# Softmax denominators of an attention and FFN kernel: products with 64 columns of ones, or with 32 columns and the queries in two strips

## The chip, the core and the metric

The kernel runs on one core of one Trainium2 chip. The metric is the device time of one execution, in microseconds (us). Before the change it is 1072.7 us, the median of 3 runs (1072.04 to 1073.84).

A core has a matrix engine (TensorE, in the profile PE, its weight loads PEld), VectorE (DVE), ScalarE (ACT) and GpSimd (POOL). TensorE multiplies a stationary operand (lhsT) with a moving one (rhs) and leaves the result in PSUM. The stationary operand's columns become the partitions of the result, so a product whose result has 64 partitions uses 64 of the array's 128 columns.

## What is computed

The reference is an attention in which a query sees only keys that are assigned to the same centroid, and then a bilinear FFN on its output:

```python
# q, k, v: (4, 8, 768, 64); centroids: (8, 16, 64)
mask = q_assign[:, :, :, None] == k_assign[:, :, None, :]
scores = scale * np.matmul(q, k.transpose(0, 1, 3, 2))
scores = np.where(mask, scores, -1000000000.0)
scores = scores - np.max(scores, axis=-1, keepdims=True)
attn = np.exp(scores)
attn = attn / (np.sum(attn, axis=-1, keepdims=True) + 1e-09)   # <- the denominators
x = np.matmul(attn, v)               # (4, 8, 768, 64) -> (3072, 512)
out = ((x @ w_a) * (x @ w_b)) @ w_out     # 512 -> 1536 -> 512
```

There are 4 batches, 8 heads and 768 queries. The change concerns the sum over the keys in `attn` and its reciprocal.

## The kernel before

The kernel treats two heads (a = 0, 1) and half of the queries (HB = 384) at a time: 16 head pairs p, two halves hf each, so 32 groups of denominators. HP = 4 head pairs make a batch. A unit is one tile of 128 keys; six units make a half. The steps of several head pairs and of the FFN are interleaved by hand, in one static order for each engine.

The probabilities lie with the keys on the partitions and the queries along the free dimension. Their sum over the keys is therefore a sum over units, done by VectorE and GpSimd, and then a sum over partitions, done by a product with ones on TensorE. Numbers such as L572 are the lines of the kernel that the profile names.

```python
ones = c["ones"] = const.tile([P, D], FP32, name="ones")      # P = 128, D = 64
nc.vector.memset(ones, 1.0)
...
# exponentials, L524; probabilities pt have 4 buffers, score tiles s in PSUM 2
pt = ptp.tile([P, 2, HB], FP32, name="pt")
nc.scalar.activation(out=pt, in_=s[:, :, 0:HB], func=AF.Exp, scale=SCALE)
...
def add_up(u):                                        # the sum over units
    p, hf, j = where(u)
    if j == 0 or j == NJ - 1 and p < HP:              # first batch: the last unit
        return                                        # is left to TensorE
    if j == 1:
        accs[p, hf] = accp.tile([P, 2, HB], FP32, name="acc")     # 2 buffers
    acc = accs[p, hf]
    for a in range(2):
        many = p >= HP and (a == 1 or j in (2, 4))
        eng = nc.gpsimd if many else nc.vector
        eng.tensor_tensor(out=acc[:, a, :],                                # L538
            in0=probs[u - 1][:, a, :] if j == 1 else acc[:, a, :],
            in1=probs[u][:, a, :], op=ALU.add)

def weigh(us):                                        # the product with v
    ...
            for a in range(2):
                nc.tensor.matmul(out=O_of[0][a * D:(a + 1) * D, 0:HB],     # L549
                                 lhsT=vs[p][:, a, j, :], rhs=probs[u][:, a, :],
                                 start=(j == 0), stop=(j == NJ - 1))

def denominators(p, hf):
    ps = ps_m.tile([P, 512], FP32, name="m")          # PSUM, 3 buffers
    acc = accs.pop((p, hf))
    terms = [acc]
    if p < HP:                                        # first batch: two terms
        terms.append(probs[p * UPP + hf * NJ + NJ - 1])
    for n, t in enumerate(terms):
        for a in range(2):
            nc.tensor.matmul(out=ps[a * D:(a + 1) * D, 0:HB], lhsT=ones,   # L572
                             rhs=t[:, a, :], start=(n == 0),
                             stop=(n == len(terms) - 1))
    den = acc[:, 0, :]
    nc.scalar.activation(out=den, in_=ps[:, 0:HB], func=AF.Copy,           # L577
                         accum_out=stat[:, n:n + 1])
```

All 64 rows of a head's result are alike, for all columns of the stationary operand are ones. `normalize` needs the reciprocal of each query's denominator on all 64 partitions of the head. It takes one reciprocal for each query instead of 64: VectorE's transpose works on blocks of 32x32, so after it a query's denominator stands in one column of a block, and only that column is inverted; the transpose back of the broadcast reciprocals spreads them over the block again.

```python
def across():
    nc.vector.transpose(out=once, in_=den)                                 # L592
def invert():
    nc.vector.reciprocal(out=inv,                                          # L595
        in_=once.rearrange("p (j t) -> p j t", t=32)[:, :, 0])
def back():
    nc.vector.transpose(out=den,                                           # L599
        in_=inv[:, :, None].broadcast_to((P, HB // 32, 32)))
def apply():
    nc.gpsimd.tensor_tensor(out=x, in0=x, in1=den, op=ALU.mult)            # L604
    ...
return [across, invert, back, apply]
```

The four steps are put into the order of the engines one at a time, each behind a piece of the FFN's products (if there is any at that time):

```python
denominators(*divmod(g // 3 - 1, 2))       # in every third group of two units
...
if halved:
    todo.extend(normalize(*ph))
...
    while len(ffn) > least and credit > 0:
        cost, piece = ffn.popleft()
        credit -= cost
        piece()                            # products of L632, L732 or L851
        if todo:
            todo.popleft()()
```

A step of the preparation of the next head pair, the similarities to the centroids, stands close by on TensorE. It already uses 32 columns of the array four times side by side:

```python
def prep_sim(p):
    ps = ps_m.tile([P, 512], FP32, name="m")
    for kq in range(4):
        nc.tensor.matmul(out=ps[32 * kq:32 * kq + 32, 0:HB],               # L353
                         lhsT=cTb[:, hp, :],                               # 128 x 32
                         rhs=qkTs[p][:, kq * HB:(kq + 1) * HB],
                         start=True, stop=True)
```

Other lines that the text names: L367 transposes these similarities on TensorE in the first batch; L428 transposes queries and keys on VectorE (768 columns); L742 adds an FFN product to its sum on VectorE; L715 combines weights on VectorE, for the FFN's products follow a scheme with fewer products and more sums; L113 is a reciprocal of one element per partition; L976 is a pair of small VectorE instructions, one for partitions 0 to 63 and one for 64 to 127.

Of the kernel before, what the change touches and what calls it, by code (L numbers as in the profile page):

```python
# [13 lines left out]
AF = mybir.ActivationFunctionType  # L14
ALU = mybir.AluOpType
# [20 lines left out]
def kernel(  # L36
# [89 lines left out]
    with ExitStack() as fast:  # L126
        short_path(nc, tc, fast, c, cn, centroids_in, casts, n_far, q, k, v,
                   moe_w_a, moe_w_b, moe_w_out, out)
# [8 lines left out]
def short_path(nc, tc, ctx, c, cn, centroids_in, casts, n_far, q, k, v,  # L137
# [3 lines left out]
    B, H, S, D = q.shape  # L141
# [5 lines left out]
    NCH = DM // P  # L147
    NF = DF // P
    HB = S // 2

    def pool(name, bufs, space=None):
        kw = {} if space is None else {"space": space}
        return ctx.enter_context(tc.tile_pool(name=name, bufs=bufs, **kw))
# [21 lines left out]
    ident, identb, ones, rank = c["ident"], c["identb"], c["ones"], c["rank"]  # L175
# [171 lines left out]
    def prep_sim(p):  # L347
# [4 lines left out]
        for kq in range(4):  # L352
            nc.tensor.matmul(out=ps[32 * kq:32 * kq + 32, 0:HB],  # L353
                             lhsT=cTb[:, hp, :],
                             rhs=qkTs[p][:, kq * HB:(kq + 1) * HB],
                             start=True, stop=True)
        if by_blocks(p):
            sims[p] = ps
            return
        t = simp.tile([P, HB], FP32, name="sim")  # L360
        nc.scalar.copy(out=t, in_=ps[:, 0:HB])
        sims[p] = t
# [48 lines left out]
    def prep_by_blocks(p):  # L411
# [19 lines left out]
        def sims_across():  # L431
            v.transpose(out=sim.rearrange("p g c -> p (g c)"),
                        in_=sims[p][:, 0:HB])

# [8 lines left out]
        def one_hot_across():  # L443
            v.transpose(out=ohT, in_=oh.rearrange("p g c -> p (g c)"))
            for a in range(2):
                for kq in range(4):
                    r = 32 * kq + a * NC
                    nc.sync.dma_start(
                        out=ohTs[p][a * D:a * D + NC, kq * HB:(kq + 1) * HB],
                        in_=ohT[r:r + NC, :])  # L450
# [111 lines left out]
    def denominators(p, hf):  # L562


        ps = ps_m.tile([P, 512], FP32, name="m")
        acc = accs.pop((p, hf))
        terms = [acc]
        if p < HP:
            terms.append(probs[p * UPP + hf * NJ + NJ - 1])
        for n, t in enumerate(terms):  # L570
            for a in range(2):
                nc.tensor.matmul(out=ps[a * D:(a + 1) * D, 0:HB], lhsT=ones,  # L572
                                 rhs=t[:, a, :], start=(n == 0),
                                 stop=(n == len(terms) - 1))
        den = acc[:, 0, :]
        n = 4 * p + 2 * hf
        nc.scalar.activation(out=den, in_=ps[:, 0:HB], func=AF.Copy,  # L577
                             accum_out=stat[:, n:n + 1])
        den_of[p, hf] = acc

    def normalize(p, hf):

        b, hp = divmod(p, HP)
        acc = den_of.pop((p, hf))
        den, once = acc[:, 0, :], acc[:, 1, :]
        x = xTs[b][:, hp, hf * HB:(hf + 1) * HB]
        inv = small.tile([P, HB // 32], FP32, name="inv")

        def across():
            nc.vector.transpose(out=once, in_=den)  # L592

        def invert():
            nc.vector.reciprocal(  # L595
                out=inv, in_=once.rearrange("p (j t) -> p j t", t=32)[:, :, 0])

        def back():
            nc.vector.transpose(  # L599
                out=den,  # L600
                in_=inv[:, :, None].broadcast_to((P, HB // 32, 32)))

        def apply():
            nc.gpsimd.tensor_tensor(out=x, in0=x, in1=den, op=ALU.mult)  # L604
            unchecked.append((4 * p + 2 * hf + 1, inv))

        return [across, invert, back, apply]

    def check_inverses():
        while unchecked:  # L610
# [376 lines left out]
    for g in range(NG + 3):  # L987
        p, l = divmod(g, GPP)
# [16 lines left out]
        if g % 3 == late and 0 < g - late:  # L1005
            denominators(*divmod(g // 3 - 1, 2))
# [15 lines left out]
        if halved:  # L1022
            todo.extend(normalize(*ph))
# [24 lines left out]
    def some_ffn(n):  # L1048
        for _ in range(n):
# [15 lines left out]
    ps = ps_m.tile([P, 512], FP32, name="m")  # L1065
    nc.tensor.matmul(out=ps[0:1, 0:1], lhsT=far_off, rhs=ones[:, 0:1],
                     start=True, stop=True)
# [227 lines left out]
```

## Time and profile before

The profile is of one execution, with a span of 1071.4 us and a mean granted TensorE clock of 0.995.

| part of the profile | number |
|---|---|
| VectorE busy | 713.7 us |
| L572, products with ones, TensorE | 160 records |
| L592 and L599, VectorE's transposes | 32 each, 566 and 575 ns mean |
| L595, VectorE's reciprocal | 32, 221 ns mean |
| L577, ScalarE's copy of the denominators | 32, 488 ns mean |
| L604, GpSimd's product | 32, 1039 ns mean |
| L353, similarities, TensorE | 128 records |

How to read it: a record of TensorE is busy from the issue of a product to its modelled end, and records overlap, so that the busy time of a line of TensorE counts the same moment more than once. What a group of products costs is the distance between its first start and the first start of the next group. An fp32 product leaves two records. On VectorE, an instruction that waits for nothing can start a little before the one ahead of it has ended. "Idle before, releaser" names the instruction whose end let a waiting one go on.

### The profile page before, as it was taken

How to read it: one execution, taken by the hardware profiler on the slowest of the kernel's cores; microseconds unless marked ns; L12 is line 12 of the kernel's file. 1: busy time of each engine (PE TensorE's matmuls, PEld its weight loads, DVE VectorE, ACT ScalarE, POOL GpSimd, SP SyncE). 2: the span in 40 equal slices, each digit the busy share in tenths (PEclk: the TensorE clock that was granted, in tenths of full speed). 3: DMA queues.
4: the chain of work that ended last, by engine and by line, in shares of the span. 5: the costliest groups of instructions: out<-in, count | busy, mean ns of one | idle time of the engine just before them, and what ended most of it. 6: DMA issues, size and time to landing. Idle time of an engine off the chain costs nothing.

```text
span 1071.4 us, 13000 instructions
## 1 busy us (share of the span) xinstructions
PE 1046.6 (98%) x4719; PEld 602.5 (56%) x4719; DVE 713.7 (67%) x1396; ACT 259.0 (24%) x500; POOL 355.8 (33%) x329
## 2 busy tenths in 40 slices
PE   5999999999999999999999999999999999999997
PEld 3444455454556665454545766455455687555686
DVE  5888978787857537766666746667665745676762
ACT  4565423333322221122121221221212200000000
POOL 1221244454542323434444522344344410222200
PEclk8999999999999999999999999999999999999999
DMA  4335352525120120202030030300000000000001
GB/s 140 91 83 91 90 123 82 123 83 136 66 49 15 31 53 14 45 4 45 2 45 2 24 65 13 56 1 19 1 4 1 6 30 25 0 1 1 0 30 33
DMA packets 120504, 46.18 MB, mean 43 GB/s; under 512 B 106608, under 2 KB 115824, under 8 KB 120432
## 3 DMA queue, kind: packets, MB, share of 16 engines
q1 hardware_dynamic: 119456, 43.40, 17.9%
q10 hardware_dynamic: 976, 1.87, 0.5%
q8 instruction: 39, 0.64, 0.3%
q14 instruction: 33, 0.27, 0.1%
HBM read 37.78 MB, written 6.29 MB: 41 GB/s over the span
## 4 chain that ended last, share of the span: by engine, by line
PE 93%; DVE 5%; issue 0%; DMA 0%; POOL 0%; ACT 0%; DVEq 0%; POOLq 0%
PE m L732 30%; PE m L851 19%; PE O L549 12%; PE m L632 12%; PE s L517 11%; PE s L508 4%; PE m L572 3%; PE m L353 1%; DVE raw L693 1%; PE m L337 1%; DVE raw L715 1%; DVE xT L693 0%; DVE acc L538 0%; PE m L399 0%; DVE size L693 0%
## 5 line engine op out<-in xcount | busy, mean ns | idle before, releaser
L524 ACT ACTIVATE pt<-s 128x768 f32<-128x768 f32 x192 | 145.3, 809 | 313.7 <-PE s L517 258.5
L538 POOL TENSOR_TENSOR acc<-acc,pt 128x384 f32<-128x384 f32 x144 | 151.9, 1068 | 59.8 <-ACT pt L524 43.5
L747 POOL TENSOR_TENSOR h<-h,ha 128x384 f32<-128x384 f32 x72 | 72.6, 1016 | 235.8 <-DVE ha L742 234.3
L549 PE MATMUL O<-pt,v 128*64 128x384 f32 x768 | 145.1, 499 | 0.0
L517 PE MATMUL s<-qkT 64*128 64x384 f32 x768 | 140.7, 486 | 0.0
L742 DVE TENSOR_TENSOR ha<-ha,m 128x384 f32<-128x384 f32 x126 | 66.8, 546 | 74.1 <-PE m L732 73.3
L742 DVE TENSOR_TENSOR h<-h,m 128x384 f32<-128x384 f32 x126 | 67.4, 549 | 68.5 <-PE m L732 67.7
L538 DVE TENSOR_TENSOR acc<-acc,pt 128x384 f32<-128x384 f32 x96 | 72.8, 787 | 35.4 <-POOL acc L538 35.0
L549 PEld LDWEIGHTS O<-pt,v 128*64 128x64 f32 x768 | 46.6, 136 | 86.4 <-issue 82.1
L604 POOL TENSOR_TENSOR xT<-xT,acc 128x384 f32<-128x384 f32 x32 | 33.3, 1039 | 169.7 <-DVE acc L599 139.2
L517 PEld LDWEIGHTS s<-qkT 64*128 64x128 f32 x768 | 71.1, 188 | 32.0 <-issue 0.6
L851 PE MATMUL m<-wo_sb,h 128*128 128x256 f32 x384 | 87.5, 382 | 0.0
L851 PEld LDWEIGHTS m<-wo_sb,h 128*128 128x128 f32 x384 | 72.1, 190 | 16.0 <-issue 4.2
L732 PE MATMUL m<-raw 128*128 128x384 f32 x192 | 70.2, 488 | 0.9 <-DVE ha L742 0.9
L632 PE MATMUL m<-xT,wa_sb 128*128 128x384 f32 x192 | 67.1, 492 | 0.0
L632 PE MATMUL m<-xT,wb_sb 128*128 128x384 f32 x192 | 66.8, 491 | 0.0
L851 PE MATMUL m<-xT,h 128*128 128x256 f32 x288 | 65.4, 382 | 0.1
L851 PEld LDWEIGHTS m<-xT,h 128*128 128x128 f32 x288 | 54.1, 190 | 11.7 <-issue 1.7
L732 PE MATMUL m<-xT,wa_sb 128*128 128x384 f32 x144 | 53.0, 491 | 0.0
L732 PE MATMUL m<-xT,size 128*128 128x384 f32 x144 | 52.9, 490 | 0.0
L732 PE MATMUL m<-xT,wb_sb 128*128 128x384 f32 x144 | 52.9, 490 | 0.0
L632 PEld LDWEIGHTS m<-xT,wa_sb 128*128 128x128 f32 x192 | 35.5, 190 | 29.4 <-issue 3.6
(159 smaller groups left out, 1446.4 us busy)
## 6 DMA issues: line engine op xcount, KB each, us to landing
raw<-in_moe_w_out_dram SPq DMA_DIRECT2D x12, 512.0 KB, 3.4
raw<-in_moe_w_a_dram SPq DMA_DIRECT2D x11, 512.0 KB, 3.8
raw<-in_moe_w_b_dram SPq DMA_DIRECT2D x11, 512.0 KB, 3.6
qk<-in_q_dram SPq DMA_DIRECT2D x48, 96.0 KB, 3.1
qk<-in_k_dram SPq DMA_DIRECT2D x48, 96.0 KB, 3.6
v<-in_v_dram SPq DMA_DIRECT2D x24, 192.0 KB, 3.9
out_dram<-rest SPq DMA_DIRECT2D x24, 128.0 KB, 1.7
ohT<-oh SPq DMA_DIRECT2D x96, 12.0 KB, 1.8
```

The lines of the kernel that those rows point to most:

```text
L508: nc.tensor.matmul(out=s[:, a, 0:HB], lhsT=ohTs[p][r, S + j * P:S + (j + 1) * P], rhs=ohTs[p][r, hf * HB:(hf + 1) * HB], start=True, stop= ...
L517: nc.tensor.matmul(out=s[:, a, 0:HB], lhsT=qkTs[p][r, S + j * P:S + (j + 1) * P], rhs=qkTs[p][r, hf * HB:(hf + 1) * HB], start=False, stop ...
L524: nc.scalar.activation(out=pt, in_=s[:, :, 0:HB], func=AF.Exp, scale=SCALE)
L538: eng.tensor_tensor(out=acc[:, a, :], in0=probs[u - 1][:, a, :] if j == 1 else acc[:, a, :], in1=probs[u][:, a, :], op=ALU.add)
L549: nc.tensor.matmul(out=O_of[0][a * D:(a + 1) * D, 0:HB], lhsT=vs[p][:, a, j, :], rhs=probs[u][:, a, :], start=(j == 0), stop=(j == NJ - 1))
L572: nc.tensor.matmul(out=ps[a * D:(a + 1) * D, 0:HB], lhsT=ones, rhs=t[:, a, :], start=(n == 0), stop=(n == len(terms) - 1))
L604: nc.gpsimd.tensor_tensor(out=x, in0=x, in1=den, op=ALU.mult)
L632: nc.tensor.matmul(out=ps[:, 0:HB], lhsT=w_sb[:, ch, f * P:(f + 1) * P], rhs=xTs[b][:, ch, t0:t0 + HB], start=(ch == 0), stop=(ch == NCH - 1))
L732: nc.tensor.matmul(out=ps[:, 0:HB], lhsT=A[l][c], rhs=rhs[c], start=(c == 0), stop=(c == 1))
L742: nc.vector.tensor_tensor(out=out, in0=in0, in1=ps, op=op)
L747: nc.gpsimd.tensor_tensor(out=to, in0=to, in1=box[name], op=ALU.mult)
L851: nc.tensor.matmul(out=ps[:, 0:HN], lhsT=A[l][f // 3][:, f % 3, :], rhs=B[r][f // 2][:, f % 2, :], start=(f == 0), stop=(f == N2 - 1))
```

## The change

The denominators are computed with 32 columns of ones instead of 64. Each head's 384 queries are cut into two strips of QB = 192, and the four products (two heads, two strips) go to four quarters of the array's columns. The result then has 128 partitions of 192 columns: head 0 in quarters 0 and 1, head 1 in quarters 2 and 3. It is meant to shorten the products with ones on TensorE.

What follows has to match. ScalarE's copy and the first transpose have 192 columns. The reciprocals of a strip have to reach both quarters of the head's partitions, so that the transpose back still has 384 columns on all 64 partitions of the head: instead of one reciprocal of 128x12 there are eight of 32x6, for each head from each of two quarters to each of two quarters. They form two steps of four, one step for each head, so that a normalization has five steps instead of four.

```diff
+    QB = HB // 2
...
     for n, t in enumerate(terms):
         for a in range(2):
-            nc.tensor.matmul(out=ps[a * D:(a + 1) * D, 0:HB], lhsT=ones,
-                             rhs=t[:, a, :], start=(n == 0),
-                             stop=(n == len(terms) - 1))
-    den = acc[:, 0, :]
+            for i in range(2):
+                nc.tensor.matmul(out=ps[(2 * a + i) * 32:(2 * a + i + 1) * 32, 0:QB],
+                                 lhsT=ones[:, 0:32],
+                                 rhs=t[:, a, i * QB:(i + 1) * QB],
+                                 start=(n == 0), stop=(n == len(terms) - 1))
+    den = acc[:, 0, 0:QB]
-    nc.scalar.activation(out=den, in_=ps[:, 0:HB], func=AF.Copy,
+    nc.scalar.activation(out=den, in_=ps[:, 0:QB], func=AF.Copy,
                          accum_out=stat[:, n:n + 1])
...
-    den, once = acc[:, 0, :], acc[:, 1, :]
+    den, across32, inverse = acc[:, 0, 0:QB], acc[:, 1, 0:QB], acc[:, 0, :]
     def across():
-        nc.vector.transpose(out=once, in_=den)
-    def invert():
-        nc.vector.reciprocal(
-            out=inv, in_=once.rearrange("p (j t) -> p j t", t=32)[:, :, 0])
+        nc.vector.transpose(out=across32, in_=den)
+    def invert(a):
+        column = across32.rearrange("p (j t) -> p j t", t=32)[:, :, 0]
+        n = QB // 32
+        for i in range(2):
+            for r in range(2):
+                src, dst = 32 * (2 * a + i), 32 * (2 * a + r)
+                nc.vector.reciprocal(out=inv[dst:dst + 32, n * i:n * i + n],
+                                     in_=column[src:src + 32])
     def back():
         nc.vector.transpose(
-            out=den,
+            out=inverse,
             in_=inv[:, :, None].broadcast_to((P, HB // 32, 32)))
     def apply():
-        nc.gpsimd.tensor_tensor(out=x, in0=x, in1=den, op=ALU.mult)
+        nc.gpsimd.tensor_tensor(out=x, in0=x, in1=inverse, op=ALU.mult)
-    return [across, invert, back, apply]
+    return [across, lambda: invert(0), lambda: invert(1), back, apply]
```

## The prediction

> **What bounds the kernel now.** I read the page's busy shares first, then its chain, the waits of TensorE, and last the timeline around the line that changes.
>
> ```profile
> span 1071.4 us, 13000 instructions
> ...
> PE 1046.6 (98%) x4719; PEld 602.5 (56%) x4719; DVE 713.7 (67%) x1396; ACT 259.0 (24%) x500; POOL 355.8 (33%) x329
> ...
> PE 93%; DVE 5%; issue 0%; DMA 0%; POOL 0%; ACT 0%; DVEq 0%; POOLq 0%
> ```
>
> TensorE is busy 98% of the span and is 93% of the chain that ended last. A busy share alone could hide gaps, so I went to the waits of TensorE. Apart from the first 27 us they are a handful:
>
> ```profile
> PE m L732 <- DVE comb L715: 4.8, 3, 2.2
> PE m L572 <- DVE acc L538: 2.3, 4, 1.1
> PE m L732 <- DVE ha L742: 0.9, 2, 0.4
> ```
>
> Columns: total us, times, longest. So time taken from TensorE's queue should come off the end, unless VectorE cannot follow. L572 is the line that changes, 160 records. The timeline of TensorE (start, us, records) gives its price, by the distance from one group's start to the next one's:
>
> ```profile
> 399.92 1.51 PE L549 MATMUL O<-pt,v 128*64 128x384 f32 x8
> 401.26 0.81 PE L572 MATMUL m<-acc,ones 128*64 128x384 f32 x4
> 402.00 2.86 PE L851 MATMUL m<-wo_sb,h 128*128 128x256 f32 x12
> 404.70 2.75 PE L851 MATMUL m<-wo_sb,ha 128*128 128x256 f32 x12
> 407.29 1.45 PE L732 MATMUL m<-xT,wa_sb 128*128 128x384 f32 x4
> ```
>
> Each fp32 product is two records (two passes). The second series of L851 (full width, 12 records of 256 columns) lasts 2.59 us, from 404.70 to 407.29, so 0.84 ns per column and record: 384 columns are 0.32 us. L549 and L572 use 64 of the array's columns, and two such records (heads a=0 and a=1) run together: 4 records of L572 take 0.74 us, which is two passes of 0.32 and 0.10 us more before the next shape starts. The new form, four strips of 32 columns, exists already in L353:
>
> ```profile
> 139.32 1.51 PE L549 MATMUL O<-pt,v 128*64 128x384 f32 x8
> 140.76 0.85 PE L353 MATMUL m<-qkT,cTb 128*32 128x384 f32 x8
> 141.54 1.88 PE L632 MATMUL m<-xT,wb_sb 128*128 128x384 f32 x5
> ```
>
> Eight records in 0.78 us: four strips do run side by side, two passes of 0.32 us and 0.14 us on top. L549 before it takes 1.44 us here against 1.34 when L572 follows: again 0.10 us for a change of shape.
>
> **What the Trainium skill says.** *TensorEngine Tiling (Array Packing)*, Key Properties: tiles work independently, but changing the tiling mode, not just the tile, drains the array. The trace agrees: 0.10 us at each change of width above, none between L549 and L572, which both use 64 columns. *TensorE: Matmul & The Clock Gate*, LDWEIGHTS: a weight load costs its columns divided by 1.2, in ns. That makes 27 ns for 32 columns and 53 for 64 (estimates from that page); loads are hidden except for the first after a change of shape, and L353's first pass is indeed some 27 ns longer than its second in the trace (0.347 against 0.32 us). *VectorE: DVE Perf Modes*, Two Vector instructions with no wait between them: an instruction whose input or output starts in another quarter of the partitions than the last one's waits until all earlier ones have finished. The trace agrees:
>
> ```profile
> 10.36 0.34 DVE L976 TENSOR_SCALAR rank_far<-rank 64x16 f32<-64x16 f32 x2
> 505.18 0.48 DVE L715 TENSOR_TENSOR comb<-wb_sb 128x128 f32<-128x128 f32 x2
> ```
>
> The two L976 instructions go to partitions 0 and 64 and take 165 ns each: together 0.34, no overlap. The two of L715 start in the same quarter, take about 0.28 each, and finish in 0.48: the second starts some 0.08 before the first ends.
>
> **TensorE, step by step.** The order of instructions on TensorE is unchanged; only L572 is replaced, each product of 64x384 by two of 32x192. A pass is then 192 columns, 0.16 us, four records at once. There are 32 groups of denominators. By what precedes them in the timeline:
>
> - 13 single-term groups behind L549. Now 0.745 us. Then two passes of 0.16 and 0.14 = 0.46, and a change of shape in front that was not there, 0.10. Saved 0.185 each: **2.4 us**.
> - 10 single-term groups behind L353. Now L353 and L572 together take 1.58 us (198.47 to 200.05 in the timeline). Then both have 32 columns, the change between them goes: 0.67 for L353, 0.44 for the denominators = 1.11. Saved about 0.46 each: **4.6 us**.
> - The last group, behind L851: 0.80 to 0.46, **0.3 us**.
> - 8 groups of two terms (attention of the first batch, 33 to 131 us). Undisturbed they take 1.39 to 1.44 us and then 4 x 0.16 + 0.14 = 0.78. In five of them the sums arrive late, and the second head's sum another 0.4 to 0.5 us after the first, so that the group lasts 1.91 us (33.32 to 35.23); then some 1.25. Saved 0.65 in seven, 0.5 in the one behind L549 without a wait: **5.0 us**.
>
> Sum: 12.3 us of TensorE's 1071, 5.0 of them before 134 us.
>
> **VectorE, step by step.** Before, a normalization is a transpose (570 ns), one reciprocal (222), a transpose back (578). At 38.54, 39.13, 39.40 and 39.90 the timeline shows their starts and that of the next instruction: 1.36 us.
>
> ```profile
> 38.54 0.56 DVE L592 STREAM_TRANSPOSE acc<-acc 128x384 f32<-128x384 f32 x1
> 39.13 0.23 DVE L595 RECIPROCAL inv<-acc 128x12 f32<-128x12 f32 x1
> 39.40 0.58 DVE L599 STREAM_TRANSPOSE acc<-inv 128x384 f32<-128x384 f32 x1
> 39.90 1.79 DVE L538 TENSOR_TENSOR acc<-acc,pt 128x384 f32<-128x384 f32 x2
> ```
>
> After, the first transpose has 192 columns. From 963 ns for 768 columns (L428) and 570 for 384, 192 should take about 370: 0.20 less. The reciprocal becomes eight of 32x6. One element takes 164 ns (L113) and twelve 222, so six should take about 190. Nearly each of the eight changes its quarter of input or output, so none overlaps: 190 and 14 ns for the handover seen at L976, eight times, 1.63 us against 0.22. Net **+1.2 us per normalization**, 38 us of VectorE work in all: 714 to about 752 us, 70% of the span. ScalarE's copy of the denominators shrinks from 488 to an estimated 330 ns (384 to 192 columns); ScalarE bounds nothing.
>
> **How much of that reaches TensorE.** Where the up and down products run beside attention, VectorE mostly waits for TensorE (L742 waits 141 us in all for L732), and three PSUM buffers lie between them. Two lots of four reciprocals, 0.82 us each, go between pieces of 1.3 or 2.6 us. I take this as mostly hidden, with 1 to 2 us lost where VectorE is behind already (TensorE's waits for L715, and sums that wait for GpSimd's L604, which the longer chain puts later).
>
> The first batch is tighter: VectorE is busy 91 of the 107 us from 27 to 134. A head pair lasts 26.4 us there, in which VectorE stands idle twice for long: 1.46 us for ScalarE at 49.3 and 2.2 to 3.5 us for TensorE's L367. That is some 3.7 us. Two normalizations take 2.4 of it and a TensorE that is 1.3 us faster takes the other 1.3: VectorE comes out at its limit. The sums would then free probability tiles about a microsecond later, exponentials start later, and scores wait; part of this falls into the wait that L572 has anyway. I let a quarter of the 5.0 us go, 1.3 us.
>
> Net: 12.3 - 1.5 - 1.3 = about 9.5 us; I take 9.2, 1072.7 to 1063.5.
>
> **Rivals.**
> - *VectorE takes the gain back.* For it: +38 us of work, small instructions that cannot overlap, first batch near its limit. Against it: TensorE waits only 8 us for VectorE after 27 us. If the whole first batch turns to VectorE's pace and each later normalization costs TensorE 0.2 us, only 12.3 - 5 - 5 = 2 us remain: about 1070.
> - *Four short strips don't overlap.* For it: no record here has four strips with 192 columns, and eight weight loads per term have to be hidden behind 0.16 us passes. Against it: L353 issues its four starts within 20 ns, its loads too (109 ns each, together). If a pass took 0.24 us, the 80 passes of 40 terms would cost 80 x 0.08 = 6.4 us more: about 1070.
> - *Everything goes through*, also the waits for sums at L572: 12.3 us, about 1060.
>
> **Range and chances.** The whole TensorE saving gives 1060.4, and the two bad rivals give 1070 each; both together would be no gain. I expect most of the saving: **1063.5 us, 1059.5 to 1069** for 8 in 10. A 2% change is 21 us, more than all of L572 costs (the groups above sum to some 32 us with their waits, and at least 19 remain): faster by over 2% 0.01, within 2% 0.98, slower 0.01.
>
> **What would show it.** The denominators' groups should measure 0.44 to 0.46 us start to start (two terms 0.8 to 1.25), behind L549 with 1.44 us for L549, and L353 shortened to 0.67 where denominators follow. The reciprocals should be 256, near 190 ns, about 0.2 us apart. VectorE's busy time should rise by 30 to 40 us. TensorE's waits for VectorE should grow by 2 to 3 us, most of it before 134 us. The prediction is wrong if strips of 192 columns take more than 0.19 us a pass, or if the lines of waits show L538, L742 or L715 holding TensorE for more than some 6 us beyond today's, or if the second head's late sum stretches the two-term groups as much as before.

## The result and the profile after

The changed kernel takes 1077.0 us, the median of 6 runs (1076.85 to 1079.37), against 1072.7 us before: 1.0046 times as long, with a 95% interval of 1.0033 to 1.0058. The prediction was 1063.5 us, with a range of 1059.5 to 1069. It is wrong, and in direction too.

First the page of the changed kernel, the busy shares and the chain that ended last (lines of the kernel have moved by 1 to 9: L572 is now L575, L595 is L604, L742 is L751):

```profile
span 1075.3 us, 13547 instructions
...
PE 1042.5 (97%) x4879; PEld 601.7 (56%) x4879; DVE 747.7 (70%) x1620; ACT 255.3 (24%) x500; POOL 356.5 (33%) x329
...
PE 80%; DVE 13%; issue 3%; POOL 3%; DMA 0%; ACT 0%; DVEq 0%; POOLq 0%
```

TensorE's busy share has hardly moved, from 98 to 97%, but its share of the chain fell from 93 to 80%, and VectorE's rose from 5 to 13. The chain tells what the busy share hides.

Next the part that was to become cheaper. TensorE's timeline, for a group behind L550 (formerly L549) and one behind L354 (formerly L353):

```profile
400.49 1.51 PE L550 MATMUL O<-pt,v 128*64 128x384 f32 x8
401.93 0.53 PE L575 MATMUL m<-acc,ones 128*32 128x192 f32 x8
402.39 1.35 PE L860 MATMUL m<-wo_sb,h 128*128 128x256 f32 x5
...
317.16 0.85 PE L354 MATMUL m<-qkT,cTb 128*32 128x384 f32 x8
317.83 0.51 PE L575 MATMUL m<-acc,ones 128*32 128x192 f32 x8
318.27 2.20 PE L641 MATMUL m<-xT,wb_sb 128*128 128x384 f32 x6
```

From one group's start to the next: 0.46 us for the denominators behind L550, and 1.44 for L550 itself; 0.67 for L354 and 0.44 for the denominators behind it. These are the predicted numbers.

VectorE's normalization, in the groups by shape (busy us, mean ns):

```profile
L604 DVE RECIPROCAL inv<-acc 32x6 f32<-32x6 f32 x256 | 46.5, 182 | 3.6
L596 DVE STREAM_TRANSPOSE acc<-acc 128x192 f32<-128x192 f32 x32 | 11.7, 366 | 0.0
```

256 reciprocals of 182 ns, 0.195 us apart in the trace. The prediction had 190 ns and 0.204 us, and 370 ns for the transpose. So the cost of each part was right as well. What was wrong is how much of it reaches TensorE. The waits of TensorE (total us, times, longest):

```profile
PE m L741 <- DVE comb L724: 7.4, 3, 3.5
PE m L575 <- DVE acc L539: 3.8, 4, 2.6
PE m L354 <- DVE qkT L429: 2.8, 2, 1.7
PE m L860 <- DVE raw L834: 0.5, 2, 0.3
```

L741's wait was 4.8 us before, L575's 2.3; the other two are new. To see where time was lost I compared the start of the same product in both traces, all but the products with ones. The difference (after minus before) goes:

| at (us, before) | after minus before, us | what lies in between |
|---|---|---|
| 99.6 | -3.4 | six groups of denominators, each ahead by 0.5 to 0.65 |
| 114.3 | -0.9 | wait of L575 for the sums, then half clock |
| 198.8 | +0.4 | wait of L354 for VectorE's transposes L429 |
| 257.3 | +2.3 | the same, for the next head pair |
| 375.7 | +0.6 | gains at groups of denominators |
| 413.7 | +3.3 | wait of L741 for L724, then half clock |
| 561.0 | +1.6 | gains |
| 598.1 | +2.6 | short waits of L860 for L834 |
| 623.5 | +2.2 | gains |
| 668.0 | +4.7 | wait of L741 for L724, then half clock |
| end | +3.9 | gains and small losses |

So the gains come in steps, as predicted, and six places take more than they give. The place at 408 us shows how. Before the change, TensorE's timeline reads:

```profile
407.29 1.45 PE L732 MATMUL m<-xT,wa_sb 128*128 128x384 f32 x4
410.94 1.56 PE L732 MATMUL m<-raw,comb 128*128 128x384 f32 x4 [2.20 <-DVE comb L715]
...
412.76 1.45 PE L517 MATMUL s<-qkT 64*128 64x384 f32 x8
```

After it:

```profile
407.68 1.45 PE L741 MATMUL m<-xT,wa_sb 128*128 128x384 f32 x4
412.63 1.96 PE L741 MATMUL m<-raw,comb 128*128 128x384 f32 x4 [3.50 <-DVE comb L724]
414.52 0.82 PE L509 MATMUL s<-ohT 64*128 64x384 bf16 x4
415.13 2.41 PE L518 MATMUL s<-qkT 64*128 64x384 f32 x8
```

And VectorE's timeline ahead of that wait, before the change:

```profile
398.64 0.57 DVE L592 STREAM_TRANSPOSE acc<-acc 128x384 f32<-128x384 f32 x1
399.24 0.23 DVE L595 RECIPROCAL inv<-acc 128x12 f32<-128x12 f32 x1
399.51 0.58 DVE L599 STREAM_TRANSPOSE acc<-inv 128x384 f32<-128x384 f32 x1
401.27 0.56 DVE L538 TENSOR_TENSOR acc<-pt 128x384 f32<-128x384 f32 x1 [1.18 <-POOL xT L604]
```

After it:

```profile
399.21 0.37 DVE L596 STREAM_TRANSPOSE acc<-acc 128x192 f32<-128x192 f32 x1
399.62 1.55 DVE L604 RECIPROCAL inv<-acc 32x6 f32<-32x6 f32 x8
401.21 0.58 DVE L608 STREAM_TRANSPOSE acc<-inv 128x384 f32<-128x384 f32 x1
402.96 0.56 DVE L539 TENSOR_TENSOR acc<-pt 128x384 f32<-128x384 f32 x1 [1.17 <-ACT acc L581]
403.44 1.36 DVE L702 TENSOR_TENSOR raw<-xT 128x384 f32<-128x384 f32 x1
...
412.29 0.48 DVE L724 TENSOR_TENSOR comb<-raw,wa_sb 128x128 f32<-128x128 f32 x2
```

The normalization stands at the head of a chain: after it GpSimd scales x, then VectorE combines x (L702, eight instructions) and weights (L724), and TensorE's next product needs the result. (GpSimd's product ends at 402.93 after the change; ScalarE's copy L581, which the line names, ends 0.02 us later.) From 402.96 on nothing on VectorE waits. The reciprocals take 1.55 us here instead of 0.23, and the first transpose 0.2 us less. From the first transpose to L539 it is 3.75 us instead of 2.63, 1.12 us more, and TensorE's wait grows by 1.30, from 2.20 to 3.50: all of it passes through. (The other 0.18 us come from the start of the chain, 0.57 us later than before, while TensorE's product ahead of the wait is only 0.39 later.)

The second loss follows it. L518's eight records take 2.41 us after the wait; before the change the same product, L517, took 1.45. The windows around it (us, then busy times with counts; PEclk, the granted clock, is the third number from the end):

```profile
409.00:413.00 4.00, 0.51 (x2) 0.30 (x2) 3.90 (x13) 0.48 (x1) 0.00 (x0) 1.00 0.01 3
413.00:417.00 4.00, 4.00 (x14) 1.85 (x14) 1.60 (x5) 0.28 (x1) 0.00 (x0) 0.58 0.08 19
417.00:421.00 4.00, 4.00 (x19) 1.77 (x16) 0.49 (x2) 1.34 (x2) 0.00 (x0) 0.99 0.21 68
```

TensorE works only 0.51 of 4 us, and in the next 4 us its clock is 0.58: some 3.4 us at half. This costs 1.6 us here, and it happens at 110 and 670 us too, for at least 1.2 and 1.4 us by the table.

### The profile page after: what moved, and what is told of

It reads as the page before. It is cut to its first block, busy times and chain, and to the rows that moved or that the text cites. A ratio compares the mean times of both kernels' runs of the same rounds, so it can differ in the third digit from the quotient of the medians.

```text
span 1075.3 us, 13547 instructions
## 1 busy us (share of the span) xinstructions
PE 1042.5 (97%) x4879; PEld 601.7 (56%) x4879; DVE 747.7 (70%) x1620; ACT 255.3 (24%) x500; POOL 356.5 (33%) x329
## 4 chain that ended last, share of the span: by engine, by line
PE 80%; DVE 13%; issue 3%; POOL 3%; DMA 0%; ACT 0%; DVEq 0%; POOLq 0%
PE m L741 29%; PE m L860 18%; PE O L550 10%; PE s L518 9%; PE m L641 6%; PE s L509 3%; PE m L575 2%; PE m L354 1%; DVE acc L539 1%; DVE raw L702 1%; DVE inv L604 1%; POOL acc L539 1%; DVE raw L724 1%; PE m L338 1%; DVE ha L751 1%
## 5 line engine op out<-in xcount | busy, mean ns | idle before, releaser
L539 POOL TENSOR_TENSOR acc<-acc,pt 128x384 f32<-128x384 f32 x144 | 152.5, 1072 | 52.5 <-ACT pt L525 31.2
L550 PE MATMUL O<-pt,v 128*64 128x384 f32 x768 | 145.1, 499 | 0.0
L518 PE MATMUL s<-qkT 64*128 64x384 f32 x768 | 142.7, 491 | 0.0
L751 DVE TENSOR_TENSOR h<-h,m 128x384 f32<-128x384 f32 x126 | 67.5, 550 | 64.2 <-PE m L741 63.1
L751 DVE TENSOR_TENSOR ha<-ha,m 128x384 f32<-128x384 f32 x126 | 66.5, 544 | 62.6 <-PE m L741 60.8
L539 DVE TENSOR_TENSOR acc<-acc,pt 128x384 f32<-128x384 f32 x96 | 73.9, 798 | 41.5 <-POOL acc L539 41.1
L550 PEld LDWEIGHTS O<-pt,v 128*64 128x64 f32 x768 | 46.6, 136 | 86.7 <-issue 83.5
L518 PEld LDWEIGHTS s<-qkT 64*128 64x128 f32 x768 | 72.3, 192 | 33.0 <-issue 2.3
L860 PE MATMUL m<-wo_sb,h 128*128 128x256 f32 x384 | 87.5, 382 | 0.0
L860 PEld LDWEIGHTS m<-wo_sb,h 128*128 128x128 f32 x384 | 72.1, 190 | 14.6 <-issue 3.0
L741 PE MATMUL m<-raw 128*128 128x384 f32 x192 | 70.2, 488 | 0.9 <-DVE ha L751 0.9
L860 PE MATMUL m<-xT,h 128*128 128x256 f32 x288 | 65.4, 382 | 0.1
L860 PEld LDWEIGHTS m<-xT,h 128*128 128x128 f32 x288 | 54.1, 190 | 11.1 <-issue 2.3
L741 PE MATMUL m<-xT,wa_sb 128*128 128x384 f32 x144 | 53.1, 492 | 0.1
L741 PE MATMUL m<-xT,size 128*128 128x384 f32 x144 | 52.9, 490 | 0.0
L741 PE MATMUL m<-xT,wb_sb 128*128 128x384 f32 x144 | 52.8, 490 | 0.0
L741 PEld LDWEIGHTS m<-raw 128*128 128x128 f32 x192 | 36.1, 190 | 27.4 <-DVE ha L751 2.1
```

The lines of the kernel that those rows point to most:

```text
L518: nc.tensor.matmul(out=s[:, a, 0:HB], lhsT=qkTs[p][r, S + j * P:S + (j + 1) * P], rhs=qkTs[p][r, hf * HB:(hf + 1) * HB], start=False, stop ...
L539: eng.tensor_tensor(out=acc[:, a, :], in0=probs[u - 1][:, a, :] if j == 1 else acc[:, a, :], in1=probs[u][:, a, :], op=ALU.add)
L550: nc.tensor.matmul(out=O_of[0][a * D:(a + 1) * D, 0:HB], lhsT=vs[p][:, a, j, :], rhs=probs[u][:, a, :], start=(j == 0), stop=(j == NJ - 1))
L741: nc.tensor.matmul(out=ps[:, 0:HB], lhsT=A[l][c], rhs=rhs[c], start=(c == 0), stop=(c == 1))
L751: nc.vector.tensor_tensor(out=out, in0=in0, in1=ps, op=op)
L860: nc.tensor.matmul(out=ps[:, 0:HN], lhsT=A[l][f // 3][:, f % 3, :], rhs=B[r][f // 2][:, f % 2, :], start=(f == 0), stop=(f == N2 - 1))
```

## The experiments

The theory after this reading: what is lost is VectorE's longer normalization, at the few places where VectorE sets TensorE's pace, and the half clock that the longer waits bring. The rivals: the four strips disturb TensorE's order beyond their own time; or the fifth step, which puts the end of a normalization later in the order.

**One reciprocal instead of eight.** The strips stay on TensorE; the reciprocals of a head's other strip are left out, so half of the queries are scaled by another query's denominator.

```diff
-    for i in range(2):
-        for r in range(2):
-            ... nc.vector.reciprocal(out=inv[dst:dst + 32, n * i:n * i + n],
-                                     in_=column[src:src + 32])
+    nc.vector.reciprocal(out=inv.rearrange("p (i n) -> p i n", i=2),
+                         in_=column[:, None, :].broadcast_to((P, 2, n)))
-return [across, lambda: invert(0), lambda: invert(1), back, apply]
+return [across, invert, back, apply]
```

> The changed kernel with one reciprocal of 128x12 in place of the eight of 32x6, and four steps; the reciprocals of a head's other strip are left out, so half of the queries are scaled by another query's denominator. If VectorE's longer normalization takes the gain away (theory), TensorE keeps its 12 us: 1060 to 1062 us, no stretch at half clock after 31 us, waits of TensorE for VectorE as before the change. If the strips themselves slow TensorE down around them (rival), 1074 to 1078 us as in the changed kernel.

Measured: 1060.4 us, 0.9892 of the kernel before (0.9865 to 0.9919). Its waits of TensorE and its reciprocal:

```profile
PE m L739 <- DVE comb L722: 4.7, 3, 2.2
PE m L575 <- DVE acc L539: 2.5, 5, 0.9
...
L601 DVE RECIPROCAL inv<-acc 128x12 f32<-128x12 f32 x32 | 7.1, 221 | 0.4
```

The waits are those of before, and the time is that of before less the 12.3 us worked out for TensorE (1060.4). The rival of the strips falls: strips alone give everything they promise, in every place of the table above. In this run's trace TensorE is 4.4 us ahead of the kernel before at 99.6 us, 5.3 at 114, 8.3 at 407 and, behind the wait there, still 8.3 at 411. So a gain of TensorE passes these places; what it does not survive is VectorE's longer normalization.

**Eight reciprocals alone.** The kernel before, with 64-column products, and eight reciprocals of 32x6 in two steps.

```diff
-    nc.vector.reciprocal(out=inv, in_=once.rearrange(...)[:, :, 0])
+    for i in range(2):
+        for r in range(2):
+            src, dst = 32 * (2 * a + i), 32 * (2 * a + r)
+            nc.vector.reciprocal(out=inv[dst:dst + 32, n * i:n * i + n],
+                                 in_=column[src:src + 32, n * i:n * i + n])
```

> The kernel before with its 64-column products, but eight reciprocals of 32x6 in two steps instead of one of 128x12; computes the same. Theory: the loss of some 16 us (12 saved on TensorE, 4 slower in the end) is all VectorE's, a little more than in the changed kernel since the first transpose keeps 384 columns: 1084 to 1092 us. Milder form of the theory (VectorE has more slack when TensorE is slower): 1078 to 1084. Rival (strips): 1073 to 1075.

Measured: 1089.3 us, 1.0147 (1.0126 to 1.0167). Its waits are nearly those of the changed kernel, though TensorE is 12 us slower:

```profile
PE m L738 <- DVE comb L721: 7.4, 3, 3.5
PE m L572 <- DVE acc L538: 3.6, 4, 2.4
PE m L353 <- DVE qkT L428: 2.8, 2, 1.7
```

The loss was thus measured twice, without strips (1089.3 - 1073.0 = 16.3 us) and with them (1077.0 - 1060.4 = 16.6). A slower TensorE gives VectorE no slack at those places, for there VectorE's own chain sets the pace.

**All eight in one step.** `return [across, lambda: (invert(0), invert(1)), back, apply]`, else as changed.

> The changed kernel with its eight reciprocals in one step instead of two, so that a normalization is put into the order in four steps as before. If the later place of the last two steps is a good part of the loss (rival), 1066 to 1073 us. If it is the time of the eight reciprocals (theory), 1075 to 1079, for they are executed all the same.

Measured: 1077.3 us, 1.0036 (1.0026 to 1.0046). It differs from the changed kernel by no more than the noise, so the place in the order is not the cause; together with the two runs before, that leaves the time of the instructions.

**Eight reciprocals that need not wait for each other.** As in the first experiment the other strip is left out, but eight reciprocals of 128x6 stand there, all starting at partition 0.

```diff
-    nc.vector.reciprocal(out=inv[dst:dst + 32, n * i:n * i + n],
-                         in_=column[src:src + 32])
+    nc.vector.reciprocal(out=inv[:, n * i:n * i + n], in_=column)
```

> The changed kernel with eight reciprocals of 128x6 which all start at partition 0, instead of eight of 32x6 which change their quarter; as in e1 the other strip's reciprocals are left out. If a change of quarter is what keeps them from overlapping, they come about 0.11 us apart instead of 0.195, so 0.7 us less for each normalization: 1066 to 1070 us. If eight small instructions cost the same wherever they start: 0.195 us apart and 1075 to 1079.

Measured: 1069.3 us, 0.9957 (0.9940 to 0.9974). The group:

```profile
L603 DVE RECIPROCAL inv<-acc 128x6 f32<-128x6 f32 x256 | 30.1, 170 | 0.4
```

They are 0.109 us apart in the trace against 0.195, with four times the lanes. Of the 16.6 us about half, the step from 1.0046 to 0.9957 of the kernel before (9.5 us), comes from the change of quarter between instructions, and the rest from there being eight. In the trace two of the changed kernel's three stretches at half clock are gone too, and are part of this step.

**Fillers against the half clock.** Products whose results nobody reads, put into the waits. The first try took its PSUM buffer from the pool of the FFN products:

```diff
+def fill(lhsT, rhs, n):
+    ps = ps_m.tile([P, 512], FP32, name="m")
+    for _ in range(n):
+        nc.tensor.matmul(out=ps[:, 0:HB], lhsT=lhsT, rhs=rhs, start=True, stop=True)
```

> The changed kernel with products on TensorE whose results nobody reads, put where TensorE falls to half clock: two (1.3 us) before the denominators of the fourth head pair's first half, four (2.6 us) before the second product after each of the combinations of batches 1 and 2. They lie in waits of 2.8 to 3.7 us. If half clock behind long waits is part of the loss, TensorE keeps full clock and gains about 1.6 us at each of three places: 1072 to 1073.5 us, granted clock 0.995. If it is not, or other waits take it up: 1076 to 1080.

Measured: 1078.6 us, 1.0046 (1.0030 to 1.0063): nothing gained. (The waits that the expectation gives as 2.8 to 3.7 us are 2.6 to 3.5 in the trace.) The half clock at 110 and 413 us is gone in its trace. At 110 us TensorE gains 2.1 us, but 1.65 of them are lost again by 131 us. At the two combinations the fillers could start only when VectorE had emptied a buffer of that pool, and pushed the product that matters back by 1.8 and 3.4 us. So this run doesn't tell what the half clock costs. The second try uses a score tile (`ps_s`), three products, only at the two combinations:

> The changed kernel with three products (1.9 us) that nobody reads, before the second product after the combinations of batches 1 and 2, in a score tile of PSUM, which is free then. (In the filler run before, the fillers had to wait for the PSUM buffers that VectorE was late to empty.) If half clock behind the waits of 3.7 us costs time by itself, full clock saves about 1.5 us at each of the two places: 1073 to 1075 us against 1077. If time won there is lost again at VectorE's next chain: 1076 to 1078.

Measured: 1074.7 us, 1.0009 (1.0002 to 1.0015). The windows around 413 us now, and TensorE's timeline with the fillers (L707):

```profile
411.00:415.00 4.00, 2.43 (x8) 1.06 (x6) 3.68 (x13) 0.00 (x0) 0.00 (x0) 1.00 0.03 8
415.00:419.00 4.00, 4.00 (x23) 1.79 (x23) 1.02 (x2) 1.51 (x2) 0.00 (x0) 1.00 0.17 49
...
410.09 2.10 PE L707 MATMUL s<-xT,wa_sb 128*128 128x384 f32 x6
413.76 0.59 PE L747 MATMUL m<-raw,comb 128*128 128x384 f32 x1 [1.57 <-DVE comb L730]
```

Full clock here, and the ratio falls from 1.0046 to 1.0009, some 4 us; by the medians it is 2.3 us. The trace shows 3.0 us won at the two places, and 1.0 us lost at 259 us, where a stretch at half clock comes that the changed kernel's trace hasn't. So the half clock is a cost of its own on top of the wait, about a fifth of the 16.6 us at these two places.

**Another engine for the spreading: ScalarE.** TensorE in strips, VectorE as before, and ScalarE copies each strip from PSUM to both quarters of its head:

```diff
-nc.scalar.activation(out=den, in_=ps[:, 0:QB], func=AF.Copy, accum_out=...)
+for a in range(2):
+    for i in range(2):
+        for r in range(2):       # src, dst: quarters 2a + i and 2a + r
+            nc.scalar.activation(out=den[dst, i * QB:(i + 1) * QB],
+                                 in_=ps[src, 0:QB], func=AF.Copy, ...)
```

> Strips on TensorE as in the changed kernel, but ScalarE spreads the denominators out of PSUM with eight copies of 32x192 instead of one of 128x192, each strip to both quarters of its head; VectorE's normalization is that of the kernel before, one reciprocal. Computes the same. ScalarE's work grows by some 32 x 2 us = 64 us of 255, which it has to spare. Theory: 1060 to 1064 us, faster than both. Rival, ScalarE's longer copies hold up exponentials in the first batch: 1064 to 1070.

Measured: 1093.5 us, 1.0178 (1.0150 to 1.0205), the slowest of all and outside both expectations. ScalarE's timeline for one group in the first batch, and a wait of TensorE:

```profile
35.51 0.32 ACT L586 ACTIVATE acc<-m 32x192 f32<-32x192 f32 x1 [1.23 <-PE m L575]
...
38.91 0.66 ACT L292 ACTIVATE size<-raw 128x512 f32<-128x512 f32 x1
39.59 1.51 ACT L525 ACTIVATE pt<-s 128x768 f32<-128x768 f32 x2
...
PE s L509 <- ACT pt L525: 8.7, 12, 1.9
```

The eight copies with their read-outs last from 35.51 to 38.91, 3.4 us in which ScalarE takes no exponential, and TensorE's scores wait for the exponentials. ScalarE is busy 24% of the span in the kernel before and 32% here, yet has no 3 us to give at that place. Less than half of the loss lies in the first batch: TensorE is 9.5 us behind the kernel before at 132 us and 21.5 at the end of the traces. The rest comes later, with TensorE's waits for the same copies (L743, 4.7 us, and L862, 2.1) and five stretches at half clock, and wasn't taken apart further. I made the same mistake again that the prediction made with VectorE.

**Strips in some groups only.** Both halves of the first three head pairs, and nine second halves later, with the eight reciprocals.

```diff
+def in_strips(p, hf):
+    return p < 3 or (p > 3 and hf == 1 and p % HP < HP - 1)
```

> Strips only where the changed kernel's trace shows a gain that stays: both halves of the first three head pairs, and the second halves of the later pairs that are not the last of a batch (behind L354 in the order); the other 17 groups as before the change. Computes the same. Theory (a normalization costs only where VectorE is on the chain that ends at TensorE): 6 groups save 3.4 us, 9 groups 0.46 each, less about 1: 1065 to 1068 us. Rival (every normalization costs TensorE its 1.2 us): 15 x 1.2 = 18 us lost against 7.5 saved, over 1078.

Measured: 1073.0 us, 0.9996 (0.9987 to 1.0005), between the two expectations and in neither. The first three pairs are 3.6 us ahead at 99.6 us, as expected. Then the wait for the fourth pair's sums, 1.1 us before the change, and a stretch at half clock behind it take 2.85 of it back:

```profile
PE m L628 <- DVE acc L539: 2.6, 1, 2.6
```

VectorE is the reason: in the 27 us from 85 to 112 it is busy 24.7 us in the kernel before and 26.3 here. From 60 to 85 us it is busy 24.0 us of 25 here, so earlier normalizations, far from the wait, may count as well; that was not tested. Another 1.1 us each are lost at 257 and 598 us, and 1.6 at a second stretch at half clock at 410 us.

**Another carrier: DMA.** One reciprocal of 128x6 on VectorE, then eight DMAs of 32x6 from each quarter to both of its head; the transpose back and GpSimd's product come one group of scores later. The fourth head pair and each batch's last half keep the way of before. In the later batches the normalization of a second half also starts one group of scores earlier.

```diff
+nc.vector.reciprocal(out=own, in_=column)                    # 128x6
+    ... nc.sync.dma_start(out=inv[dst:dst + 32, n * i:n * i + n],
+                          in_=own[src:src + 32, :])          # eight times
```

> Strips, with one reciprocal of 128x6 on VectorE and eight DMAs that carry it to both quarters of each head; the transpose back and GpSimd's product come one group of scores later. Only the fourth head pair and each batch's last half keep the kernel before's way. Computes the same. Theory (only VectorE's added work costs): 27 of 32 groups keep their saving, VectorE's work falls: 1060 to 1065 us. Rival: the DMAs queue behind the loads and VectorE waits for them in order, mostly in the first batch: 1068 to 1080.

Measured: 1089.6 us, 1.0144 (1.0127 to 1.0161), the rival's mechanism and worse than its range. VectorE's timeline in the first batch, and the DMA issues of SyncE (SPq), which come one after another:

```profile
84.98 0.19 DVE L601 RECIPROCAL own<-acc 128x6 f32<-128x6 f32 x1
...
96.39 0.58 DVE L613 STREAM_TRANSPOSE acc<-inv 128x384 f32<-128x384 f32 x1 [4.52 <-DMA inv<-own]
...
85.82 3.72 SPq L199 DMA_DIRECT2D qk<-in_k_dram  x4
...
90.20 4.95 SPq L609 DMA_DIRECT2D inv<-own  x8
```

The reciprocal is done at 85.17, but the loads of queries, keys and values stand ahead in SyncE's order, so that the first small DMA is issued at 90.20. Then the issues are 0.63 us apart: the eighth comes at 94.56 and lands at 96.30. VectorE waits 27 us in all at seven such places. So the issuing costs more than the landing, 1.7 us in the median; an issue from another engine was not tried. Nearly all of the loss, 21 us, lies before 132 us. After that this kernel gains 0.65 us for each head pair, 0.18 at the group behind L550 and 0.47 at the one behind L354, and loses 1.6 us once, at half clock from 685 us on.

So the next one uses strips from the second batch on:

> As the run before it, but strips only from the second batch on (21 groups), where few loads are under way. Theory: 12 groups behind L549 x 0.185 and 9 behind L354 x 0.46 to 0.65 = 6 to 8 us: 1065 to 1067 us. Rival (DMAs late): 1070 to 1078.

Measured: 1069.75 us, 0.9963 (0.9949 to 0.9977): faster than both kernels, and 2.7 us short of the expectation. VectorE is busy 712.2 us, as before the change. In its trace the gains come as worked out, and 1.6 us are lost once, at half clock behind the wait at 407 us:

```profile
411.00:415.00 4.00, 4.00 (x19) 1.81 (x20) 1.02 (x2) 1.35 (x2) 0.68 (x1) 0.63 0.23 73
```

Two fillers in a score tile there, the last run:

> The strips from the second batch on with DMAs, and two products (1.3 us) that nobody reads, in a score tile, before the second product after the combinations of batches 1 and 2. In the run without them TensorE fell to half clock at 411 us, behind a wait of 2.4 us, and lost 1.7 us of its gain there. If that goes: 1068 us, about 1.5 us less than 1069.75. If the half clock depends only on where the waits fall, and comes elsewhere: 1069 to 1070.

Measured: 1067.8 us, 0.9947 (0.9934 to 0.9961), no stretch at half clock between the start and the last microseconds. It is the best version that computes the whole: 0.5% less than the kernel before. The step from the run before it (0.9963) lies within the two intervals; that the half clock at 411 us is gone is seen in the trace.

## Why the prediction was wrong

- **TensorE's saving, 12.3 us: right.** Groups of 0.46 and 0.44 us were predicted and measured, the shape change before and behind them too, and the run with one reciprocal is 12.6 us faster than its runs of the kernel before. The rival "four short strips don't overlap" is out. One estimate on the way does not fit as it stands: a weight load of 32 columns lasts 109 ns in the trace of before (L353) and not 27, one of 64 columns 136 (L572); only the difference, 27 ns for 32 columns, agrees.
- **VectorE's work, +1.2 us per normalization, 38 us: right.** Its busy time rose from 713.7 to 747.7 us, 34 us. The rule on the change of quarter, on which this rested, is confirmed by the run with eight reciprocals that start at partition 0.
- **"How much of that reaches TensorE": the step that failed.** It allowed 1.5 us for the later batches and 1.3 for the first, 2.8 in all; measured are 16.3 and 16.6 us. The prediction named the right rival, "VectorE takes the gain back", and gave it 10 us at most. Its own sign, 6 us more of waiting at L538, L742 and L715, did not come either: these wait 4.1 us longer (7.4 instead of 4.8 us, and 3.8 instead of 2.3). The rest showed at lines it had not named (L354, 2.8 us, and L860, 0.5) and at half clock.
- The reason in it was wrong, not only its size. I took TensorE's small waits for VectorE (8 us after 27 us) as a sign of slack. They show the opposite: at each of these places VectorE is the later one already, so there every further microsecond of VectorE on the chain ahead of it is TensorE's too. (The chain itself begins with TensorE's products: with one reciprocal it begins 8.1 us earlier at 390.5 us, instead of 398.6, and TensorE's gain survives.) Between those places VectorE has slack, and its 67% is true there.
- For the first batch, "VectorE comes out at its limit" was right, but a quarter of the 5.0 us was too little. The gain was kept up to 99.6 us; 2.5 of the 3.4 us were given back at one wait and the half clock behind it.
- **The half clock** was in none of the rivals. *TensorE: Matmul & The Clock Gate*, Part 1, says that an idle window of about 3.4 us brings TensorE back to half clock, and that these windows run freely. The traces agree on the length and on the free running, but not on how idle TensorE has to be. In all thirteen traces the changes of clock lie a whole number of 3.41 us apart. Let each trace be cut into stretches of 3.41 us at these points, and TensorE's idle time in each be taken by the modelled ends of its products. From 25 us on, every stretch at full clock with 1.96 us or more of idle time is followed by one at half clock (25 of 25), and none with 1.72 us or less is; of the seven in between, three are. So it also counts where a wait falls: the 2.2 us at 408 us before the change are cut in two, 0.9 and 1.3, and no half clock follows; in the run with strips in some groups the 2.2 us at the same place fall into one stretch, and it does. I had looked at clock shares for the whole span only.
- How the loss divides is read from two traces side by side, the changed kernel's and that of the run with one reciprocal, which end 16.8 us apart: 3.4 us are lost at the place at 110 us, 2.0 at 198, 2.6 at 257, 3.0 at 408, 1.2 at 598 and 2.8 at 664, waits and half clock together. Another 1.0 us lies before 27 us, ahead of the first denominators. No run takes the six places one by one.

## What to carry to other kernels

A busy share of 98% does not say that an engine sets the pace everywhere: look for the few waits it has, and ask of each new instruction on another engine whether it lies on the chain ahead of one of them; there it costs its full time, whatever that engine's average. Before moving work to an engine with time to spare, look for the free stretch at that very place, in its timeline. Where a saving on one engine needs small instructions on another, test the two halves apart: here one was worth 12.6 us and the other cost 16.3.

## What I had not expected of the hardware

- Behind a wait of 1.7 us and more, TensorE can run at half clock for 3.41 us, which cost another 1.0 to 1.6 us each time (granted clock 0.58 in the 4 us from 413 us on).
- On ScalarE a copy of 32 partitions takes as long as one of 128: 321 ns for 32x192, 327 for 128x192, and each sum read out adds 196.
- DMAs of 0.8 KB within SBUF took 1.7 us to land in the median and 3.8 at most, but SyncE issued them 0.63 us apart, so that eight of them took 6.1 us from the first issue to the last landing (90.20 to 96.30).
